# Two recurrent attention layers with feed-forwards: softmax ends, query copies, value rows and the last feed-forward at other places

## The chip, the cores and the metric

The kernel runs on one core of one Trainium2 chip. A core has five engines that work at the same time, each through its own list of instructions in order: TensorE (PE, matmuls and transposes; its weight loads are listed as PEld), VectorE (DVE), ScalarE (ACT), GpSimd (POOL) and SyncE (SP, which here only issues DMA transfers). SBUF is the working memory with 128 partitions; PSUM is the small memory of eight banks into which PE writes and from which DVE and ACT copy results away. The metric is the device time of one execution in microseconds (us).

## What is computed

Two layers, each a memory-augmented attention over 64 segments of 32 tokens followed by a feed-forward with gated ReLU. The attention of a segment sees eight memory rows and the segment's own rows, and its first eight output rows are the memory of the next segment, so the segments of a layer form a chain.

```python
def _A_ref(x, mem0, Wq, Wk, Wv, Wo, seg_len):      # S=2048, Dm=448, H=16, Dh=256, M=8
    mem = mem0
    for s in range(n_seg):                         # 64 segments
        h = jnp.concatenate([mem, x[:, s*seg_len:(s+1)*seg_len]], axis=1)
        q, k, v = (jnp.einsum('btd,dhe->bhte', h, W) for W in (Wq, Wk, Wv))
        scores = jnp.where(mask, jnp.einsum('bhqe,bhke->bhqk', q, k) * scale, -1e9)
        o = jnp.einsum('bhqk,bhke->bhqe', _softmax(scores), v)
        o = jnp.einsum('bhte,hed->btd', o, Wo)
        mem = o[:, :M]
        outs.append(o[:, M:])
    return jnp.concatenate(outs, axis=1)
def _B_ref(x, W_gate, W_up, W_down):               # F=1792
    return (relu(x @ W_gate) * (x @ W_up)) @ W_down
for _ in range(2):
    x = x + _A_ref(_layernorm(x), mem0, Wq, Wk, Wv, Wo, seg_len)
    x = x + _B_ref(_layernorm(x), W_gate, W_up, W_down)
```

## The kernel before

**Preamble (lines 260 to 388).** Both layers use the same weights, so the kernel first multiplies them together once: A_sb = Wq·Wkᵀ for each head (the first loop over p, eight rounds) and B_sb = Wv·Wo (the second loop, eight rounds). The natural weight blocks `nat` come by DMA from SP's queue (`load_nat`), are transposed by PE (`flips`, bank `tpw`) and copied to SBUF by DVE or ACT, whichever `share` picks. The Wo blocks come from POOL's queue; POOL also clears A_sb's unused rows, `nat`'s, and the query tiles before that. A row of 448 features is three chunks of 128 and a fourth of 64 rows; the fourth chunks of two heads are packed into one 128-row chunk in places (`kd` = 3).

**Steps (lines 613 to 876).** Each of the 69 calls of `step` handles one segment of each layer. The second layer's chain (c=1) runs four segments (LAG) behind the first's (c=0): steps 0 to 3 and 64 to 67 have one chain, steps 4 to 63 have both, side by side in the matmuls' columns (80 = two times 40), and step 68 only finishes the output of segment 67. The 16 heads are worked as two halves hf=0 and hf=1. In a step PE

- projects the queries (`project`, matmuls prj): 28 tiles in five banks, in the order of BANKS, tiles 0–5, 6–11, 24–27, 12–17, 18–23. Each bank is copied to SBUF by ACT or DVE: four of them into TQ (here TQ0, TQ6, TQ12, TQ18 by their first tile) and tiles 24–27 into TZ, whose rows 0–63 and 64–127 are two copies of their own. The line that picks the engines is 556 to 559; `busy` is true for all of half hf=1 and, for hf=0, in feed steps;
- multiplies queries with keys: Sm, the scores of the memory's queries (`scores_m`), and Sx, those of the segment's queries (`scores_x`), one of each per half. Sm of hf=1 reads TQ and TZ of hf=1;
- waits for the softmax, which `softmax` splits in three parts: [0] maximum and difference on DVE, [1] the exponential on ACT, [2] the sum, the reciprocal and the product into PM or PX on DVE. m0, m1, x0, x1 are the softmaxes of Sm and Sx for the halves;
- transposes PM and PX (`flipped`, bank pps, copied to PT), multiplies with the keys' rows (`weigh_m` into ya and yb, `weigh_x` into y) and copies into Y;
- multiplies Y with B_sb (`project_out`, 84 ox matmuls per half, and `project_last`, 56 o matmuls of 64 columns).

Every odd step from 3 to 67 carries a `Feed`: layernorm, gate and up products (gps, ups), their product hh and the down product (dps) of one block of 64 rows of each layer. Step 68 is followed by the last one. Steps with a `Feed` are called feed steps, the others no-feed steps.

**Order.** PE's instructions run in the order of the program (`in_order`), and from line 881 on DVE's and ACT's do too (`InOrder`, line 96): what stands behind a waiting instruction waits with it. The PSUM banks are given out by `bank`, which takes the one that a simple clock expects to be free first. Almost all DVE and ACT instructions carry line 96 (or 151 and 153 where they are copies outside it) and all matmuls line 138 in the profile, so that groups are told apart by tile names.

Of the kernel before, what the change touches and what calls it, by code (L numbers as in the profile page):

```python
# [8 lines left out]
BF = mybir.dt.bfloat16  # L9
# [50 lines left out]
def build_kernel(ctx, tc, A_x, A_mem0, A_Wq, A_Wk, A_Wv, A_Wo, B_W_gate, B_W_up, B_W_down, out,  # L60
# [101 lines left out]
    nc.sync.dma_start(xp[1][:], x_dram[0:128])  # L162

    ident = glob.tile([P, P], BF, name="ident")
    make_identity(nc, ident[:])
# [94 lines left out]
    with tc.tile_pool(name="pre", bufs=6) as pre:  # L260
# [4 lines left out]
        for i in range(6):  # L265
            t = pre.tile([P, 4, 512], BF, name=f"nat{i}", bufs=1)
            (nc.gpsimd if i % 2 else dve).memset(t[64:128, 3, :], 0.0)
            nats.append(t)
        nc.gpsimd.memset(A_sb[64:128, 3, :, :, :], 0.0)
        nc.gpsimd.memset(A_sb[0:64, 3, :, 6:24, :], 0.0)  # L270
        for t in TQ + TZ + PX + PM + YB:
# [3 lines left out]
        def load_nat(src, p, eng):  # L275
            t = nats[nn[0] % 6]
            nn[0] += 1
            cols = slice(512 * p, 512 * (p + 1))
            eng.dma_start(t[:, 0:3, :], src[0:384, cols].rearrange("(k p) n -> p k n", p=P))
            eng.dma_start(t[0:64, 3, :], src[384:448, cols])  # L280
            if src is Wq:
                eng.dma_start(t[64:128, 3, :], src[384:448, cols])
            return t

        spent = {dve: 0.0, act: 0.0}

        def share(dst, src, n, per):
            cost = {dve: 60 + n * per[0], act: 170 + n * per[1]}
            eng = min(cost, key=lambda e: spent[e] + cost[e])
            spent[eng] += cost[eng]  # L290
            evac(eng, dst, src)

        def flips(src, p, name):
            nat = load_nat(src, p, nc.sync)
            o = pre.tile([P, 4, 512], BF, tag="tT", name=name)

            def half(e2):
                tp = bank([P, 2, 512], BF, "tpw")
                for e in range(2):
                    for kd in range(4):  # L300
                        tr(tp[:, e, kd * 128:(kd + 1) * 128],
                           nat[:, kd, (2 * e2 + e) * 128:(2 * e2 + e + 1) * 128], ident[:])
                share(o[:, 2 * e2:2 * e2 + 2, :], tp[:], 1024, (0.6, 0.82))

            return o, [lambda: half(0), lambda: half(1)]
# [10 lines left out]
        def first_rows(xn0):  # L316
# [9 lines left out]
            set_mem(0, mem0T[:].unsqueeze(2), (0,))  # L326

        ready, todo = queue(0)
        for u in todo:
            u()  # L330
# [35 lines left out]
        for p in range(NP):  # L366
            hf, p4 = divmod(p, 4)
            vT = ready
            ready, todo = flips(Wv, p + 1, "vT") if p + 1 < NP else (None, [])
            wo = pre.tile([P, 4, DM], BF, tag="wo", name="wo", bufs=4)  # L370
            nc.gpsimd.dma_start(wo[:], Wo[:, 4 * p:4 * p + 4, :])
            for eo in range(2):
                for kd in range(3):
                    bps = bank([P, 512], F32, "bps")
                    for t in range(2):
                        e = 2 * eo + t
                        mm(bps[:, 0:DM], vT[:, e, kd * 128:(kd + 1) * 128], wo[:, e, :],
                           start=(t == 0), stop=(t == 1))
                    share(B_sb[:, hf, tidx(kd, eo, p4), 0:DM], bps[:, 0:DM], DM, (1.28, 0.85))
                    if kd == 1 and todo:  # L380
                        todo.pop(0)()
            bps = bank([P, 512], F32, "bps")
            for t in range(2):
                for eo in range(2):
                    e = 2 * eo + t
                    mm(bps[64 * eo:64 * eo + 64, 0:DM], vT[:, e, 384:448], wo[:, e, :],
                       start=(t == 0), stop=(t == 1), tile_position=(0, 64 * eo))
            share(B_sb[:, hf, 24 + p4, 0:DM], bps[:, 0:DM], DM, (1.28, 0.85))
# [45 lines left out]
    class Feed:  # L434
# [38 lines left out]

        def gate_up(self, u):
            n = self.n
            k = min(4, FT - 4 * u)
            for W_sb, ps in zip((Wu_sb, Wg_sb), self.ps[u]):
                for e in range(k):
                    f = 4 * u + e
                    for kd in range(3):  # L480
                        mm(ps[:, e, n], W_sb[:, kd, f * 128:(f + 1) * 128], xT[:, kd, n],
                           start=False, stop=(kd == 2), skip_group_check=True)
                let_go(ps)
            ups, gps = self.ps[u]
            ut = p_ut.tile([P, 4, 128], BF, tag="ut")
            act.copy(ut[:, 0:k, n], ups[:, 0:k, n])
            dve.scalar_tensor_tensor(out=hh[:, 4 * u:4 * u + k, n], in0=gps[:, 0:k, n], scalar=0.0,
                                     in1=ut[:, 0:k, n], op0=ALU.max, op1=ALU.mult)

        def down(self):  # L490
            i = self.i
            dps = bank([P, 512], F32, "dps")
            for f in range(FT):
                mm(dps[:, 0:DM], hh[:, f, :], Wd_sb[:, f, :], start=(f == 0), stop=(f == FT - 1))
            if self.first:
                dve.tensor_tensor(self.nx[TB:P, :], dps[TB:P, 0:DM], self.x[TB:P, :], op=ALU.add)
                self.st = row_stats(self.nx)
                nc.sync.dma_start(xa[(i + 2) % 3][0:TB, :], self.nx[TB:P, :])
            if self.second:
                dve.tensor_tensor(self.x[0:TB, :], dps[0:TB, 0:DM], self.x[0:TB, :], op=ALU.add)  # L500
                nc.sync.dma_start(out_dram[block(i - LAG // BLK)], self.x[0:TB, :])
# [36 lines left out]
    def project(hf, chains, hb, j, banks, pre={}, busy=False, first=None, inside=None):  # L538

        n = L * len(chains)  # L540
        for i0, k in banks:
# [12 lines left out]
            if i0 < 24:  # L554
                T = TQ[hf][:].rearrange("p g u w -> p g (u w)")[:, :, 16 * i0:16 * (i0 + k)]
                parts = [(act if (i0 != 6 if busy and hf else i0 % 12) else dve, slice(0, P), T)]
            else:
                parts = [(act if busy else dve, slice(0, 64), TZ[hf][0:64, :, 0:64]),
                         (act, slice(64, 128), TZ[hf][64:128, :, 64:128])]
# [53 lines left out]
    def step(g, ff, pre, late):  # L613
# [5 lines left out]
        cols = [(0, 32) if c == 0 else (48, 80) for c in xs] + [(32, 40) if c == 0 else (40, 48) for c in ms]  # L619
        lo, hi = min(a for a, _ in cols), max(b for _, b in cols)  # L620
        end = g == nsteps - 1
        if g == nsteps:
# [3 lines left out]
        def ox_open():  # L626

            nonlocal ox
            ox = bank([P, 3, W], F32, "ox", 1400, hold=True) if not end else None

# [43 lines left out]
        def weigh_x(hf, hk, PT):  # L674
# [14 lines left out]
            for c in chains:  # L689
                keep(act if c == 0 else dve, c, 0, y1[c][:])  # L690
            y2 = {c: bank([P, 384], F32, f"y2_{c}", 1300) for c in chains}
# [9 lines left out]
            for c in chains:  # L701
                eng = dve if c or len(chains) == 1 else act
                keep(eng, c, 16, y2[c][:, 0:256])
                keep(eng, c, 24, y2[c][:, 256:384])

        def project_out(hf, t0, t1):

            if end:
                return
            for t in range(t0, t1):  # L710
# [5 lines left out]
        def project_last():  # L716

            if end:
                return
            o3 = bank([P, W], F32, "o3", 1200)  # L720
# [26 lines left out]
        def finish():  # L747
# [5 lines left out]
            if g == nsteps:  # L753
                act.copy(OT[:, 0:3, 0:SEG], ox[:, :, XO[1]:XO[1] + SEG])
                dve.tensor_copy(OT[:, 0:3, SEG:TB], ox[:, :, XL:XL + SEG])
                return
# [9 lines left out]
        if not chains:  # L766
            late()
            ox_open()
# [12 lines left out]
        if ff is not None:  # L781
            ff.norm()
        pre1 = {}
        if late is not None:
            pre1 = project_early(1, chains, hb, j)
            late()
# [32 lines left out]
        x1 = scores_x(1)  # L819
        x0[0]()  # L820
        if ff is not None:
            ff.open_rows((0, 1))
# [26 lines left out]
        else:  # L849
# [3 lines left out]
            m1[2]()  # L853
            late_flip = 23 if len(chains) == 2 else 26
            project_out(0, 0, late_flip)
            pm = flipped(PM[1], 1, "m1") if ms else None
            x0[2]()
            project_out(0, late_flip, NT)
            weigh_m(1, hk, pm)
            x1[0]()  # L860
            x1[1]()
            next_piece()
            project_last()
            x1[2]()
            project_out(1, 0, 10)
# [4 lines left out]
            project_out(1, 25, NT)  # L870
        if not end:
            finish()
        nxt = active(g + 1)
# [7 lines left out]
    dve.on = act.on = True  # L881
    pre, late = {}, None
    for g in range(nsteps + 1):
        if g == LAG - 1:
            set_mem(LAG, mem0T[:].unsqueeze(2), (1,))
        i = (g - 3) // 2
        pre, late = step(g, Feed(i) if g % 2 and 0 <= i < nblk + LAG // BLK - 1 else None, pre, late)

    ff = Feed(nblk + LAG // BLK - 1)
    ff.residual()  # L890
    ff.norm()
    ff.xposed()
    ff.xposed_out()
    for us in ((0, 1), (2, 3)):
        ff.open_rows(us)
# [61 lines left out]
```

## Time and profile before

| | us |
|---|---|
| three runs | 1611.59, 1609.84, 1609.4 (median 1609.84) |
| the profiled execution | 1608.87 |
| its span in the trace | 1606.8 |
| first loop of the preamble (A_sb) | about 9 to 49 |
| second loop (B_sb) | about 49 to 79 |
| 60 two-chain steps, in 30 pairs of a no-feed and a feed step | 45.58 per pair |
| last no-feed step and last `Feed` | 1581 to 1607 |
| mean granted PE clock | 0.995 of full |

The profile's page gives for each engine the busy time and its share of the span, then groups of instructions by line and tile, and the chain of work that ended last. Busy time is a sum over instructions, a chain is a path through them: an engine with a low share can still stand on the path. The granted clock is the share of full speed that PE is given; where it is 0.5 each matmul takes about twice its time. In a timeline, "[0.40 <-PE prj L138]" says that the engine stood idle 0.40 us before this row and that PE's prj ended the wait. Rows such as "x2" stand for two instructions one after the other.

### The profile page before, as it was taken

Reading aid. Unit: us, or ns where it says so; the run is one execution under the profiler, and the core shown is the slowest. Engines: PE = TensorE matmul, PEld = TensorE weight load, DVE = VectorE, ACT = ScalarE, POOL = GpSimd, SP = SyncE. Lnnn points to the kernel's source line nnn. Section 1 sums busy time; section 2 is a strip of 40 time slices with the busy share of each in tenths; the row PEclk is TensorE's granted clock in tenths of the full one; section 3 lists DMA queues with packets and bytes.
Section 4 is the critical chain, followed back from the end, with each engine's and each line's share of the span. In section 5 each row is a group of like instructions: output and inputs, shape, how many; then the busy total and the mean of one; then the engine's idle time right before and its main releaser. Section 6 shows DMA issues by size and latency. Waiting matters only on the chain.

```text
span 1606.8 us, 89746 instructions
## 1 busy us (share of the span) xinstructions
PE 1583.5 (99%) x41152; PEld 1453.7 (90%) x41152; DVE 1135.4 (71%) x3721; ACT 753.7 (47%) x2057; POOL 87.8 (5%) x176
## 2 busy tenths in 40 slices
PE   8999999999999999999999999999999999999997
PEld 6698899999999999999999999999999999999886
DVE  7766777777677777776777777767777777766774
ACT  5744444554444444544445445444444455444432
POOL 6200000000000000000000000000000000000000
PEclk9989999999999999999999999999999999999999
DMA  9430000000000000000000000000000000000000
GB/s 262 131 108 25 8 9 9 4 9 10 9 9 9 9 9 7 7 9 10 9 9 9 9 9 4 10 9 9 9 9 9 9 5 8 9 8 7 6 7 6
DMA packets 26778, 33.11 MB, mean 21 GB/s; under 512 B 3352, under 2 KB 24736, under 8 KB 26400
## 3 DMA queue, kind: packets, MB, share of 16 engines
q1 hardware_dynamic: 25312, 23.70, 5.3%
q8 instruction: 321, 5.26, 1.4%
q0 software_dynamic: 1088, 3.68, 0.8%
q14 instruction: 57, 0.47, 0.1%
HBM read 23.70 MB, written 1.84 MB: 16 GB/s over the span
## 4 chain that ended last, share of the span: by engine, by line
PE 92%; DVE 5%; POOL 2%; issue 1%; ACT 0%; POOLq 0%; ACTq 0%
PE prj L138 30%; PE ox L138 24%; PE ups L138 7%; PE dps L138 6%; PE gps L138 5%; PE y L138 4%; PE o L138 4%; PE Sx L138 3%; PE pps L146 2%; PE Sm L138 2%; PE bps L138 1%; DVE Y L96 1%; PE kps L146 1%; PE tps L146 1%; PE tpw L146 1%; PE aps L138 1%
## 5 line engine op out<-in xcount | busy, mean ns | idle before, releaser
L138 PE MATMUL prj<-hT,A_sb 128*128 128x80 bf16 (+3 forms) x15232 | 542.2, 199 | 0.0
L138 PEld LDWEIGHTS <-A_sb 128*128 128x128 bf16 (+1 forms) x15232 | 499.6, 99 | 21.9 <-issue 0.6
L138 PEld LDWEIGHTS <-B_sb 128*128 128x128 bf16 (+1 forms) x15232 | 494.6, 103 | 19.2 <-issue 5.7
L138 PE MATMUL ox<-Y,B_sb 128*128 128x80 bf16 (+4 forms) x11424 | 439.2, 199 | 0.0
L96 ACT CAST TQ<-prj 128x480 bf16<-128x480 f32 (+1 forms) x380 | 180.5, 496 | 82.3 <-PE prj L138 75.5
L96 DVE CAST Y<-y 128x256 bf16<-128x256 f32 (+2 forms) x400 | 160.9, 457 | 45.7 <-PE y L138 45.4
L96 ACT CAST Y<-y 128x256 bf16<-128x256 f32 (+1 forms) x368 | 128.4, 420 | 92.5 <-PE y L138 92.5
L96 ACT ACTIVATE se<-se 128x80 f32<-128x80 f32 (+1 forms) x270 | 81.9, 303 | 185.6 <-DVE se L96 181.5
L138 PE MATMUL gps<-xT,Wg_sb 128*128 128x128 bf16 (+3 forms) x1904 | 134.6, 216 | 0.0
L138 PE MATMUL ups<-xT,Wu_sb 128*128 128x128 bf16 (+3 forms) x1904 | 133.2, 217 | 0.5 <-DVE xT L96 0.5
L96 DVE CAST TQ<-prj 128x480 bf16<-128x480 f32 (+1 forms) x228 | 128.6, 573 | 5.8 <-PE prj L138 5.3
L96 ACT CAST TZ<-prj 64x320 bf16<-64x320 f32 (+2 forms) x264 | 97.8, 381 | 40.1 <-PE prj L138 23.5
L96 DVE SCALAR_TENSOR_TENSOR hh<-gps,ut 128x512 bf16<-128x512 f32 (+2 forms) x136 | 80.5, 593 | 50.2 <-PE ya L138 40.0
L138 PEld LDWEIGHTS <-hk 40*128 40x128 bf16 (+1 forms) x1950 | 100.3, 96 | 14.7 <-issue 2.1
L138 PEld LDWEIGHTS <-Wu_sb 128*128 128x128 bf16 (+1 forms) x1904 | 105.7, 97 | 8.0
L138 PEld LDWEIGHTS <-Wg_sb 128*128 128x128 bf16 (+1 forms) x1904 | 107.5, 97 | 0.5 <-issue 0.5
L96 ACT COPY os<-o 64x16 f32<-64x16 f32 (+3 forms) x135 | 25.7, 190 | 165.3 <-PE o L138 164.0
L96 DVE TENSOR_REDUCE ssum<-se 128x2 f32<-128x80 f32 (+1 forms) x270 | 73.3, 272 | 38.3 <-ACT se L96 38.3
L138 PE MATMUL dps<-Wd_sb,hh 128*128 128x448 bf16 x476 | 95.7, 353 | 0.0
L222 POOL TENSOR_SCALAR rstd<-mv 128x1 f32<-128x1 f32 x67 | 14.8, 221 | 1465.3 <-DVE mv L96 1465.3
L138 PEld LDWEIGHTS <-TQ 128*128 128x128 bf16 x1938 | 87.1, 97 | 6.5 <-ACT TQ L96 1.1
L138 PE MATMUL y<-PT,hk 40*128 40x256 bf16 (+1 forms) x1280 | 90.4, 249 | 0.8 <-ACT Y L96 0.6
(116 smaller groups left out, 1939.5 us busy)
## 6 DMA issues: line engine op xcount, KB each, us to landing
wo<-in_A_Wo_dram POOLq DMA_DIRECT2D x8, 448.0 KB, 5.7
nat<-in_A_Wq_dram SPq DMA_DIRECT2D x8, 384.0 KB, 5.4
nat<-in_A_Wk_dram SPq DMA_DIRECT2D x8, 384.0 KB, 5.0
nat<-in_A_Wv_dram SPq DMA_DIRECT2D x8, 384.0 KB, 4.9
xa<-in_A_x_dram SPq DMA_DIRECT2D x32, 56.0 KB, 2.6
xa<-xp SPq DMA_DIRECT2D x32, 56.0 KB, 1.9
out_dram<-xa SPq DMA_DIRECT2D x32, 56.0 KB, 2.0
xp<-in_A_x_dram SPq DMA_DIRECT2D x30, 56.0 KB, 2.4
```

Source lines behind the costliest of these rows:

```text
L96: r = f(*a, **k)
L138: in_order(nc.tensor.matmul(out, lhsT, rhs, **k))
L146: in_order(nc.tensor.transpose(out, src, idn))
L222: nc.gpsimd.tensor_scalar(out=rstd[:], in0=mv[:, 1:2], scalar1=EPS, scalar2=None, op0=ALU.add)
```

## The change

- **Query copies.** In half hf=1 of every step tiles 6–11 (TQ6) are copied by ACT instead of DVE, and TZ's lower rows by DVE instead of ACT. Half hf=0 is as before.
- **Softmax ends.** In no-feed steps x0[2] moves from before the last ox matmuls of hf=0 to after x1[1], and x1[2] from behind `project_last` to ahead of it.
- **One-chain steps.** In step 0 the fourth chunks' projections of both halves are now made ahead of time (`project_early`), as in the other steps; copies of y go to ACT or DVE in another way where there is one chain; `late_flip` is chosen by the width of ox.
- **Step 0.** ox has columns from 0 on (40 columns) instead of the eight memory columns alone.
- **Preamble.** Eight matmuls on a tile of zeros ahead of the first transposes, and four more between those of Wq and Wk. The last 64 rows of Wv are loaded beside those of Wk into rows 64–127 of the fourth chunk, transposed with them and kept in `v3`; Wv's own blocks then need three transposes per 128 columns instead of four. The `nat` blocks are not cleared any more, and of A_sb only rows 64–127 of tiles 24–27. `share` counts when the engines will be free by the simple clock.
- **End.** Step 67 makes gate and up of units 0 and 1 only, and all of its remaining attention work. Units 2 and 3 and the down product of its `Feed` come after step 68, the down product in two parts, around the last `Feed`'s residual and row statistics. The last `Feed` multiplies its down product as pairs of column tiles (even f into rows 0–63 of the bank, odd f into rows 64–127), and the two halves are added after a copy by ACT.

```diff
+        def keep_warm(n):
+            junk = bank([P, 512], F32, "junk")
+            for _ in range(n):
+                mm(junk[:], still[:, 0:128], still[:], start=True, stop=True)
...
-            (nc.gpsimd if i % 2 else dve).memset(t[64:128, 3, :], 0.0)
...
-        nc.gpsimd.memset(A_sb[64:128, 3, :, :, :], 0.0)
-        nc.gpsimd.memset(A_sb[0:64, 3, :, 6:24, :], 0.0)
+        nc.gpsimd.memset(A_sb[64:128, 3, :, 24:NT, :], 0.0)
...
+            if src is Wv:
+                return t
             eng.dma_start(t[0:64, 3, :], src[384:448, cols])
-            if src is Wq:
-                eng.dma_start(t[64:128, 3, :], src[384:448, cols])
+            eng.dma_start(t[64:128, 3, :], (Wq if src is Wq else Wv)[384:448, cols])
...
+                n = 3 if src is Wv else 4
                 for e in range(2):
-                    for kd in range(4):
+                    for kd in range(n):
                         tr(tp[:, e, kd * 128:(kd + 1) * 128],
...
+                if src is Wk:
+                    share(v3[:, p, 2 * e2:2 * e2 + 2, :], tp[:, :, DM:512], 128, (0.6, 0.82))
...
+        keep_warm(8)
         ready, todo = queue(0)
-        for u in todo:
+        for k, u in enumerate(todo):
+            if k == 2:
+                keep_warm(4)
             u()
...
-                    mm(bps[64 * eo:64 * eo + 64, 0:DM], vT[:, e, 384:448], wo[:, e, :],
+                    mm(bps[64 * eo:64 * eo + 64, 0:DM], v3[:, p, e, :], wo[:, e, :],
...
+        def down_part(self, f0, f1):
+            if f0 == 0:
+                self.dps = bank([P, 512], F32, "dps", hold=True)
+            dps = self.dps
+            for f in range(f0, f1):
+                if self.first:
+                    mm(dps[:, 0:DM], hh[:, f, :], Wd_sb[:, f, :], start=(f == 0), stop=(f == FT - 1))
+                else:
+                    r = slice(64 * (f % 2), 64 * (f % 2) + 64)
+                    mm(dps[r, 0:DM], hh[:, f, 0:TB], Wd_sb[:, f, :], start=(f < 2), stop=(f >= FT - 2),
+                       tile_position=(0, r.start), skip_group_check=True)
...
+            if self.second and not self.first:
+                other = main.tile([P, DM], F32, tag="other", name="other")
+                act.copy(other[0:TB, :], dps[TB:P, 0:DM])
+                dve.tensor_tensor(self.x[0:TB, :], dps[0:TB, 0:DM], self.x[0:TB, :], op=ALU.add)
+                dve.tensor_tensor(self.x[0:TB, :], other[0:TB, :], self.x[0:TB, :], op=ALU.add)
...
-                parts = [(act if (i0 != 6 if busy and hf else i0 % 12) else dve, slice(0, P), T)]
+                parts = [(act if busy and hf or i0 % 12 else dve, slice(0, P), T)]
             else:
-                parts = [(act if busy else dve, slice(0, 64), TZ[hf][0:64, :, 0:64]),
+                parts = [(act if busy and not hf else dve, slice(0, 64), TZ[hf][0:64, :, 0:64]),
                          (act, slice(64, 128), TZ[hf][64:128, :, 64:128])]
...
+        if g == 0:
+            lo = 0
...
             for c in chains:
-                keep(act if c == 0 else dve, c, 0, y1[c][:])
+                keep(act if c == 0 or len(chains) == 1 else dve, c, 0, y1[c][:])
...
-                eng = dve if c or len(chains) == 1 else act
+                eng = (act if hf else dve) if len(chains) == 1 else dve if c else act
...
             if g == nsteps:
-                act.copy(OT[:, 0:3, 0:SEG], ox[:, :, XO[1]:XO[1] + SEG])
+                dve.tensor_copy(OT[:, 0:3, 0:SEG], ox[:, :, XO[1]:XO[1] + SEG])
...
-        pre1 = {}
+        pre1 = project_early(1, chains, hb, j)
         if late is not None:
-            pre1 = project_early(1, chains, hb, j)
             late()
...
+        if end:
+            ff.open_rows((0, 1))
+            x0[1]()
+            x1[0]()
+            x1[1]()
+            x0[2]()
+            ff.products(0)
+            ff.products(1)
+            px0 = flipped(PX[0], 2, "x0", act)
+            x1[2]()
+            ff.gated(0)
+            ff.gated(1)
+            weigh_x(0, hk, px0)
+            px1 = flipped(PX[1], 2, "x1", act)
+            weigh_x(1, hk, px1)
+            return {}, None
...
-            late_flip = 23 if len(chains) == 2 else 26
+            late_flip = 23 if hi - lo == W else 26
             project_out(0, 0, late_flip)
             pm = flipped(PM[1], 1, "m1") if ms else None
-            x0[2]()
             project_out(0, late_flip, NT)
             weigh_m(1, hk, pm)
             x1[0]()
             x1[1]()
+            x0[2]()
+            x1[2]()
             next_piece()
             project_last()
-            x1[2]()
...
-    pre, late = {}, None
+    pre, late = project_early(0, active(0), hTb[0], 0), None
...
     ff = Feed(nblk + LAG // BLK - 1)
+    fed.open_rows((2, 3))
     ff.residual()
+    for u in (2, 3):
+        fed.products(u)
+    for u in (2, 3):
+        fed.gated(u)
+    fed.down_part(0, 8)
     ff.norm()
+    fed.down_part(8, FT)
     ff.xposed()
     ff.xposed_out()
+    fed.down_out()
     for us in ((0, 1), (2, 3)):
```

More of the change, by code (lines that the diff above doesn't have):

```diff
@@ L162, in build_kernel @@
     nc.sync.dma_start(xp[1][:], x_dram[0:128])
+    still = glob.tile([P, 512], BF, name="still")
+    nc.vector.memset(still[:], 0.0)
+    def keep_warm(n):
+        junk = bank([P, 512], F32, "junk")
+        for _ in range(n):
+            mm(junk[:], still[:, 0:128], still[:], start=True, stop=True)
     ident = glob.tile([P, P], BF, name="ident")
@@ L279, in load_nat @@
             eng.dma_start(t[:, 0:3, :], src[0:384, cols].rearrange("(k p) n -> p k n", p=P))
+            if src is Wv:
+                return t
             eng.dma_start(t[0:64, 3, :], src[384:448, cols])
-            if src is Wq:
-                eng.dma_start(t[64:128, 3, :], src[384:448, cols])
-            return t
-        spent = {dve: 0.0, act: 0.0}
+            eng.dma_start(t[64:128, 3, :], (Wq if src is Wq else Wv)[384:448, cols])
+            return t
+        v3 = pre.tile([P, NP, 4, 64], BF, name="v3", bufs=1)
+        until = {dve: 0.0, act: 0.0}
         def share(dst, src, n, per):
             cost = {dve: 60 + n * per[0], act: 170 + n * per[1]}
-            eng = min(cost, key=lambda e: spent[e] + cost[e])
-            spent[eng] += cost[eng]
+            ends = {e: max(until[e], now[0]) + cost[e] for e in cost}
+            eng = min(ends, key=ends.get)
+            until[eng] = ends[eng]
             evac(eng, dst, src)
@@ L298, in half @@
                 tp = bank([P, 2, 512], BF, "tpw")
+                n = 3 if src is Wv else 4
                 for e in range(2):
-                    for kd in range(4):
+                    for kd in range(n):
                         tr(tp[:, e, kd * 128:(kd + 1) * 128],
                            nat[:, kd, (2 * e2 + e) * 128:(2 * e2 + e + 1) * 128], ident[:])
-                share(o[:, 2 * e2:2 * e2 + 2, :], tp[:], 1024, (0.6, 0.82))
+                n = DM if src is Wk else 128 * n
+                share(o[:, 2 * e2:2 * e2 + 2, 0:n], tp[:, :, 0:n], 2 * n, (0.6, 0.82))
+                if src is Wk:
+                    share(v3[:, p, 2 * e2:2 * e2 + 2, :], tp[:, :, DM:512], 128, (0.6, 0.82))
             return o, [lambda: half(0), lambda: half(1)]
@@ L474, in gate_up, with products @@
         def gate_up(self, u):
+            self.products(u)
+            self.gated(u)
+        def products(self, u):
             n = self.n
@@ L483, in gate_up, with gated @@
                 let_go(ps)
+        def gated(self, u):
+            n = self.n
+            k = min(4, FT - 4 * u)
             ups, gps = self.ps[u]
@@ L488, in gate_up, with down_out @@
                                      in1=ut[:, 0:k, n], op0=ALU.max, op1=ALU.mult)
+        def down_part(self, f0, f1):
[9 more added lines that the diff above has]
+                       tile_position=(0, r.start), skip_group_check=True)
+            if f1 == FT:
+                let_go(dps)
         def down(self):
[L491 to L494, printed above, removed]
+            self.down_part(0, FT)
+            self.down_out()
+        def down_out(self):
+            i, dps = self.i, self.dps
             if self.first:
@@ L498, in down @@
                 nc.sync.dma_start(xa[(i + 2) % 3][0:TB, :], self.nx[TB:P, :])
-            if self.second:
+            if self.second and not self.first:
[3 more added lines that the diff above has]
+                dve.tensor_tensor(self.x[0:TB, :], other[0:TB, :], self.x[0:TB, :], op=ALU.add)
+                nc.sync.dma_start(out_dram[block(i - LAG // BLK)], self.x[0:TB, :])
+            elif self.second:
                 dve.tensor_tensor(self.x[0:TB, :], dps[0:TB, 0:DM], self.x[0:TB, :], op=ALU.add)
@@ L628, in ox_open @@
             nonlocal ox
-            ox = bank([P, 3, W], F32, "ox", 1400, hold=True) if not end else None
+            ox = bank([P, 3, W], F32, "ox", 1400, hold=True)
         def hk_make():
@@ L706, in project_out @@
         def project_out(hf, t0, t1):
-            if end:
-                return
             for t in range(t0, t1):
@@ L716, in project_last @@
         def project_last():
-            if end:
-                return
             o3 = bank([P, W], F32, "o3", 1200)
@@ L766, in step @@
         if not chains:
-            late()
             ox_open()
@@ L870, in step @@
             project_out(1, 25, NT)
-        if not end:
-            finish()
+        finish()
         nxt = active(g + 1)
@@ L886, in build_kernel @@
         i = (g - 3) // 2
-        pre, late = step(g, Feed(i) if g % 2 and 0 <= i < nblk + LAG // BLK - 1 else None, pre, late)
+        if g % 2 and 0 <= i < nblk + LAG // BLK - 1:
+            fed = Feed(i)
+            pre, late = step(g, fed, pre, late)
+        else:
+            pre, late = step(g, None, pre, late)
     ff = Feed(nblk + LAG // BLK - 1)
+    fed.open_rows((2, 3))
     ff.residual()
+    for u in (2, 3):
[3 more added lines that the diff above has]
+    fed.down_part(0, 8)
     ff.norm()
+    fed.down_part(8, FT)
     ff.xposed()
     ff.xposed_out()
+    fed.down_out()
     for us in ((0, 1), (2, 3)):
```

## The prediction

> **What bounds the kernel now.** I read the busy shares first, then the chain of waits by engine, then the timeline of one pair of steps, and last the two ends of the run.
>
> ```profile
> PE 1583.5 (99%) x41152; PEld 1453.7 (90%) x41152; DVE 1135.4 (71%) x3721; ACT 753.7 (47%) x2057; POOL 87.8 (5%) x176
> ...
> PE 92%; DVE 5%; POOL 2%; issue 1%; ACT 0%; POOLq 0%; ACTq 0%
> ```
>
> TensorE (PE) is busy for 99% of the span and carries 92% of the chain. It works in program order, so a change gains by fewer matmuls, by a faster clock, or by a shorter wait, and it loses by whatever makes PE wait. Between 89 and 1575 us the same two steps repeat: a no-feed step and a feed step, together 45.58 us, 30 times over. The place that decides this change is the last part of the query copies of half hf=1, here in a no-feed step (start, duration, engine, operation):
>
> ```profile
> 1428.15 0.27 ACT L96 ACTIVATE se<-se 128x80 f32<-128x80 f32 x1
> 1428.82 0.86 ACT L96 CAST TZ<-prj 64x320 bf16<-64x320 f32 x2 [0.40 <-PE prj L138]
> 1429.71 1.02 ACT L96 CAST TQ<-prj 128x480 bf16<-128x480 f32 x2
> ...
> 1429.12 0.24 DVE L96 TENSOR_TENSOR PM<-se,rs 128x80 bf16<-128x80 f32 x1
> 1429.28 0.65 DVE L96 CAST TQ<-prj 128x480 bf16<-128x480 f32 x1
> ...
> 1430.66 0.20 PE L138 MATMUL Sm<-hT,TZ 128*128 128x80 bf16 x1
> 1430.78 0.21 PE L138 MATMUL Sm<-hT,TQ 128*128 128x80 bf16 x1
> ```
>
> ScalarE (ACT) copies both halves of TZ and then TQ12 and TQ18. PE's Sm, the score matmuls of this half, starts 1430.78 just behind the end of TQ18 at 1430.73: 0.120 us between its last two matmuls where 0.035 is the usual step. ACT is on the critical path here with no slack, though it is busy only 47% of the span. VectorE (DVE) is held by the softmax end PM until 1429.28.
>
> **The change part by part.**
>
> **1. Query copies, hf=1.** TQ6 goes from DVE to ACT, and TZ's lower half goes from ACT to DVE. Does ACT's upper half then wait for DVE's lower half? The no-feed steps of half hf=0 already split TZ this way, and the view of the tile TZ shows what happens there:
>
> ```profile
> L96 ACT CAST TZ<-prj x264: 178/420/433, 81.9 to 1575.7; 64x320 bf16<-64x320 f32 x105, 64x32 bf16<-64x32 f32 x27
> ...
> L96 DVE CAST TZ<-prj x40: 182/483/483, 81.4 to 1556.7; 64x320 bf16<-64x320 f32 x30, 64x32 bf16<-64x32 f32 x5, 64x128 bf16<-64x128 f32 x5
> ...
>   DVE TZ L96: 14.2, 32
> ```
>
> ACT waited 32 times, 14.2 us in all, and starts 0.035 us after DVE ends. In hf=1 DVE's half stands behind PM, and TQ12 and TQ18 are queued behind the waiting ACT copy. No-feed step: DVE free at 1429.28, TZ lower 0.48 → 1429.77, lag 0.035, TZ upper 0.42 → 1430.22, TQ12 0.56 plus 0.02 → 1430.80, TQ18 0.56 less its 0.10 overlap → 1431.26, PE 0.055 later at 1431.32 instead of 1430.78: **+0.54**. TQ6 itself fits ACT's gap between the exponential at 1428.15 and the TZ bank. Feed step, by the same sum from DVE's 1402.37: 1402.85; 0.09 for ACT's start, since its own bank is late too, and 0.42 → 1403.36; TQ12 1403.94; TQ18 1404.40; PE 1404.455 instead of 1404.015: +0.44, and +0.42 with the lag taken between 0.035 and 0.09: **+0.42**. No trace row has this split in hf=1: if the existing Sm waits (0.085 and 0.137 us) vanish inside the new ones the two are 0.455 and 0.283; a second 0.09 lag makes 0.6 and 0.5.
>
> The Trainium skill, page "PSUM — Partial Sum Buffer", section "PSUM bank collisions raise a hardware error", says two engines may access one bank at the same time if they touch different quadrants of partitions, as rows 0–63 and 64–127 are. By it the two copies could run side by side; this trace shows ACT waiting each time, so the sum takes the wait (the other case is rival A).
>
> **2. Softmax ends in no-feed steps.** x0's second half moves behind x1's first, and x1's second ahead of the 56 matmuls o. Now those matmuls lose time:
>
> ```profile
> 1416.50 1.19 PE L138 MATMUL o<-Y,B_sb 128*64 128x80 bf16 x56
> ...
> 1434.61 1.45 PE L138 MATMUL o<-Y,B_sb 128*64 128x80 bf16 x56
> ...
> 1434.65 0.32 DVE L96 TENSOR_TENSOR PX<-se,rs 128x160 bf16<-128x160 f32 x1
> 1434.90 0.42 DVE L96 CAST Y<-ya 128x256 bf16<-128x256 f32 x1
> ```
>
> 1.45 against 1.19 in the feed step: DVE copies ya to Y only behind PX, and the last o matmuls need Y. With x0's end out of the way the copy runs some 0.3 earlier: **−0.24**. But PX0 is then ready about 1436.76, and its transposes, now at 1437.08 and 0.24 earlier after the change, start 0.15 after PX's end (as in the tail): 1436.91 against 1436.84, so **+0.08** (0 to 0.2).
>
> A pair thus costs 0.54 − 0.24 + 0.08 + 0.42 = +0.80; ×30 = **+24.0 us** (bounds 0.48 and 0.96 a pair: 14 to 29).
>
> **3. One-chain steps** (five no-feed, two feed). The TZ wait costs about +0.53 and +0.52; the earlier projection, the moved ends and the rebalanced Y copies take about 0.36 off a no-feed step: 5×0.16 + 2×0.52 = **+1.8** (−1 to +4).
>
> **4. Preamble.** PE's first work waits 5.5 us for the first weights and runs at half clock until 11.3; eight junk matmuls of 512 columns fill that wait: −0.9. The A_sb memsets on GpSimd (POOL), 6.06 + 3.93 us, become about 0.9: the stall behind them at 16.64 (PE restarts at 17.48) goes, −0.6, and one before tps at 26.4, −0.55. SP issues as many DMAs as before. POOL, though, reaches the four Wo loads (448 KB each, before from 23.3) at 13 to 17 us, ahead of Wq/Wk loads on a DMA system already 92–95% busy, and Wk's loads carry 64 KB more: p=4's Wq lands some 1.3 after it is needed: **+1.3** (0 to 4). Phase two drops four of 16 transposes of Wv per p: 8×4×56 ns = **−1.8**. Projecting early in step 0 saves **−0.6**. Last, step 0's ox has eight columns, and the clock drops (columns: us, then busy and count of PE, PEld, DVE, ACT, POOL; clock; DMA share; GB/s):
>
> ```profile
> 86.40:89.80 3.40, 3.22 (x108) 3.02 (x105) 2.63 (x12) 0.92 (x3) 0.00 (x0) 1.00 0.53 160
> 89.80:100.00 10.20, 10.20 (x295) 9.58 (x293) 4.97 (x20) 3.70 (x14) 0.00 (x0) 0.50 0.37 116
> 106.90:117.10 10.20, 9.94 (x372) 9.32 (x370) 6.53 (x28) 4.99 (x20) 0.00 (x0) 1.00 0.26 71
> ```
>
> The same stretch takes 10.46 us in step 0 and 8.24 in step 1, which has 40 columns and full clock; step 0 gets 40: **−2.2** (0 to −2.4). Together −0.9 −0.6 −0.55 +1.3 −1.8 −0.6 −2.2 = **−5.4** (−9 to −0.5).
>
> The Trainium skill, "TensorE: Matmul & The Clock Gate", section "What's actually happening", has the clock fall after an idle window of about 3.4 us. PE was issuing without a break ahead of the drop, so by that rule wider columns need not help and the sum would be 2.2 higher; the two rows above speak for the columns.
>
> **5. Tail.** The second half of the feed-forward in step 67 (0.28 + 1.05 + 2.65 us of PE, less its waits) moves under the last row statistics, where PE now idles and then runs cold:
>
> ```profile
> 1591.54 0.40 PE L146 MATMUL otp<-ident,OT 128*128 128x128 bf16 x4 [0.68 <-DVE OT L96]
> ...
> 1594.69 0.44 PE L146 MATMUL tps<-ident,xn 128*128 128x128 bf16 x4 [2.75 <-DVE xn L96]
> ...
> 1595.10:1598.40 3.30, 2.79 (x59) 2.72 (x59) 0.85 (x2) 0.39 (x2) 0.00 (x0) 0.50 0.00 0
> ```
>
> Step 68's ox then starts at 1581.8 instead of 1584.69: −2.9. OT's copies side by side: −0.1. The clock stays up over gate and up: −1.2 at most, taken as −0.9. The last down as seven pairs of column tiles: −1.2, against an added ACT copy and a second add, +0.65: −0.55. Together **−4.4** (−6 to −2.5).
>
> **Sum**: 24.0 + 1.8 − 5.4 − 4.4 = **+16.0 us**, made against the profiled execution of 1608.87 (span 1606.8 and 2.1 around it): 1624.9. That execution lies 0.97 under the median of the runs, 1609.84, to which my forecast is put: **1625.8 us**.
>
> **Rivals.**
> *A, the halves run side by side.* Then no wait is added, the copies are merely balanced and the pair keeps −0.24 + 0.08 = −0.16: −4.9 − 0.8 − 5.4 − 4.4 = −15.5, **1594 us**. For it: the halves are different rows of bank and tile. Against it: 32 waits on just this pair of copies. Chance 0.12; this is the rival on the other side, and it decides once ACT's wait per step falls below 0.3 us.
> *B, half the delay is absorbed*, because DVE and ACT catch up while PE stands and the later waits of the pair shrink: 12 + 1.8 − 9.8 = +4, **1614**, down to no change. Against it: beside those counted, PE shows hardly a wait in the pair that could shrink. Chance 0.13, of which 0.05 within 0.2%.
> *C, Wo's early loads hold up Wq by 4 us* instead of 1.3: **1628.5**. For it: in the trace a Wk load issued at 26.90 behind Wo's landed 35.58. Chance 0.12.
> *D, clocks not gained* in step 0 and tail: +2.2 + 0.9, **1629**. Chance 0.13.
>
> **How the numbers follow.** The forecast itself, 1620 to 1628, has 0.50. A measurement of this kernel tells a change from none at about 0.2%, 3.2 us. Faster by more: A, 0.12. Within: 0.05 of B. Slower: 0.83. The range, **1611 to 1631**, leaves out A and the corners of C and D together with the upper bound of part 1. Slower cases hold most of it, so it has one side.
>
> **What would show it.** Right: ACT's TZ row with DVE TZ as its releaser about 100 times instead of 32, Sm's last matmul in each pair late by some half microsecond, o's 56 matmuls at 1.19 in both steps, a pair of about 46.4 us. Wrong: a pair of 45.4 or less (A); PE waiting for nat between 24 and 30 us for more than 2 us (C); clock 0.50 after 89 us or in the last gate and up (D).

## The result and the profile after

The changed kernel takes 1623.69 us (median of four runs, 1623.19 to 1626.59) where the kernel before took 1609.62 beside it: a ratio of 1.0089 with a 95% interval of 1.0071 to 1.0106. The profiled execution took 1623.19, its span is 1621.1: 14.3 us more than the 1606.8 of before. The page's busy shares and the chain of waits by engine:

```profile
PE 1587.5 (98%) x41132; PEld 1448.0 (89%) x41132; DVE 1122.7 (69%) x3706; ACT 751.4 (46%) x2090; POOL 77.7 (5%) x172
...
PE 73%; DVE 15%; ACT 7%; issue 2%; POOL 2%; DMA 1%; SPq 0%; ACTq 0%; POOLq 0%
```

PE has twenty matmuls fewer and still carries less of the chain, 73% instead of 92%: the path now runs through DVE and ACT in every step. The view of the tile TZ, and who waited for it:

```profile
L96 ACT CAST TZ<-prj x188: 181/422/434, 82.6 to 1594.8; 64x320 bf16<-64x320 f32 x150, 64x32 bf16<-64x32 f32 x19, 64x128 bf16<-64x128 f32 x19
...
L96 DVE CAST TZ<-prj x116: 175/476/484, 82.1 to 1594.3; 64x320 bf16<-64x320 f32 x90, 64x32 bf16<-64x32 f32 x13, 64x128 bf16<-64x128 f32 x13
...
  DVE TZ L96: 74.3, 95
```

ACT waits for DVE's half 95 times and 74.3 us in all, where it was 32 times and 14.2. The timelines of ACT, DVE and PE at the same place as before (a no-feed step, hf=1):

```profile
1449.15 0.42 ACT L96 CAST TZ<-prj 64x320 bf16<-64x320 f32 x1 [0.92 <-DVE TZ L96]
1449.60 1.02 ACT L96 CAST TQ<-prj 128x480 bf16<-128x480 f32 x2
...
1448.48 0.24 DVE L96 TENSOR_TENSOR PM<-se,rs 128x80 bf16<-128x80 f32 x1
1448.64 0.47 DVE L96 CAST TZ<-prj 64x320 bf16<-64x320 f32 x1
...
1450.25 0.21 PE L138 MATMUL Sm<-hT,TZ 128*128 128x80 bf16 x1
1450.67 0.21 PE L138 MATMUL Sm<-hT,TQ 128*128 128x80 bf16 x1 [0.21 <-ACT TQ L96]
```

ACT stands idle 0.92 us, TQ12 and TQ18 follow late, and PE's last Sm matmul starts 0.42 us behind the one before it, which itself is 0.23 late; the usual step is 0.035. Over all steps the gaps between these matmuls beyond the usual step have a median of 0.62 us in no-feed and 0.58 in feed steps, where it was 0.09 and 0.14. From the starts of kps, one per step, the no-feed step grew from 18.26 to 18.56 us and the feed step from 27.32 to 27.76. The second part of the change shows in the same step, in PE's and DVE's timelines:

```profile
1454.50 1.19 PE L138 MATMUL o<-Y,B_sb 128*64 128x80 bf16 x56
1456.72 0.29 PE L146 MATMUL pps<-ident,PX 128*128 128x128 bf16 x2
...
1454.50 0.42 DVE L96 CAST Y<-ya 128x256 bf16<-128x256 f32 x1 [0.42 <-PE ya L138]
1456.34 0.32 DVE L96 TENSOR_TENSOR PX<-se,rs 128x160 bf16<-128x160 f32 x1
```

The 56 matmuls o take 1.19 instead of 1.45: the copy into Y is no longer behind PX. The transposes of PX start 0.06 after PX's end. The early part is told by PE's waits of the first 90 us, and by step 0 in the windows (us, then busy and count of PE, PEld, DVE, ACT, POOL; clock; DMA share; GB/s):

```profile
PE tpw L146 <- DMA nat<-in_A_Wk_dram: 3.1, 2, 2.8
...
89.80:100.00 10.20, 9.75 (x352) 9.11 (x352) 5.73 (x24) 5.18 (x20) 0.00 (x0) 1.00 0.41 127
```

PE stood 2.8 us for a block of Wk that had landed behind the Wo loads, while step 0 runs at full clock where it had 0.50. In the tail PE's timeline shows the wait for xn:

```profile
1610.52 0.44 PE L146 MATMUL tps<-ident,xn 128*128 128x128 bf16 x4 [0.27 <-DVE xn L96]
1614.76 1.51 PE L138 MATMUL dps<-Wd_sb,hh 128*64 128x448 bf16 x14
```

It fell from 2.75 to 0.27, and the last down product from 2.81 to 1.51. The 14.3 us by stretch, cut at the kps starts:

| stretch | before | after | difference | forecast |
|---|---|---|---|---|
| start to first kps | 80.56 | 81.30 | +0.7 | −2.5 |
| steps 0 to 3 | 68.96 | 67.07 | −1.9 | −1.8 |
| the two-chain steps (remainder) | | | +21.9 | +24.0 |
| steps 64 to 66 | 56.12 | 54.33 | −1.8 | +0.8 |
| step 67's kps to the end | 35.80 | 31.10 | −4.7 | −4.4 |

### The profile page after: what moved, and what is told of

Same layout as the page of the kernel before. It is cut to its first block, busy times and chain, and to the rows that moved or that the text cites. A ratio compares the mean times of both kernels' runs of the same rounds, so it can differ in the third digit from the quotient of the medians.

```text
span 1621.1 us, 89762 instructions
## 1 busy us (share of the span) xinstructions
PE 1587.5 (98%) x41132; PEld 1448.0 (89%) x41132; DVE 1122.7 (69%) x3706; ACT 751.4 (46%) x2090; POOL 77.7 (5%) x172
## 4 chain that ended last, share of the span: by engine, by line
PE 73%; DVE 15%; ACT 7%; issue 2%; POOL 2%; DMA 1%; SPq 0%; ACTq 0%; POOLq 0%
PE ox L138 25%; PE prj L138 14%; PE ups L138 7%; PE dps L138 5%; PE gps L138 5%; PE o L138 5%; DVE Y L96 4%; ACT TQ L96 4%; PE y L138 3%; ACT TZ L96 2%; PE Sx L138 2%; DVE TZ L96 2%; PE pps L146 1%; DVE rs L96 1%; PE bps L138 1%
## 5 line engine op out<-in xcount | busy, mean ns | idle before, releaser
L138 PE MATMUL ox<-Y,B_sb 128*128 128x80 bf16 (+3 forms) x11424 | 440.1, 199 | 1.3 <-issue 1.3
L96 ACT CAST TQ<-prj 128x480 bf16<-128x480 f32 (+1 forms) x456 | 213.0, 496 | 72.6 <-PE prj L138 68.9
L96 ACT CAST Y<-y 128x512 bf16<-128x512 f32 (+2 forms) x392 | 136.6, 419 | 95.4 <-PE y L138 95.3
L96 DVE CAST Y<-y 128x256 bf16<-128x256 f32 x376 | 151.3, 457 | 42.1 <-PE y L138 41.9
L138 PEld LDWEIGHTS <-TQ 128*128 128x128 bf16 x1938 | 91.8, 97 | 34.0 <-ACT TQ L96 28.1
L96 ACT CAST TZ<-prj 64x320 bf16<-64x320 f32 (+2 forms) x188 | 70.2, 383 | 78.0 <-DVE TZ L96 74.3
L138 PE MATMUL dps<-Wd_sb,hh 128*128 128x448 bf16 (+1 forms) x476 | 93.1, 353 | 0.0
L96 DVE CAST TQ<-prj 128x480 bf16<-128x480 f32 (+2 forms) x152 | 85.8, 573 | 6.2 <-PE prj L138 5.7
```

Source lines behind the costliest of these rows:

```text
L96: r = f(*a, **k)
L138: in_order(nc.tensor.matmul(out, lhsT, rhs, **k))
```

## The experiments

**One part at a time.** Four kernels ask whether ACT's wait is the loss, and whether the two parts of the pair add up. The first turns only the order of the two TZ copies in hf=1:

```diff
                          (act, slice(64, 128), TZ[hf][64:128, :, 64:128])]
+                if busy and hf:
+                    parts.reverse()
```

> The changed kernel with one thing turned: in half hf=1 ACT's copy of TZ's upper rows stands in the program before DVE's copy of the lower rows, so that it has nothing of DVE's to wait for. Theory W (the loss is ACT's wait for DVE, with TQ12 and TQ18 queued behind it): Sm's extra gaps fall from 0.61 and 0.58 us a step to about 0.09 and 0.14, a pair from 46.33 to 45.35, the whole by 30 x 0.98 + 7 x 0.5 = 33 to about 1591 us. Theory L (ACT simply has too much work once TQ6 is its own): the copies are the same ones on the same engines, a pair stays above 46.0 and the time above 1614.

Measured: 1594.5 us (ratio to before 0.9905, 0.989 to 0.992), a pair 45.34. The copies, their number and their engines are those of the changed kernel; 29 us hang on which of two instructions stands first. ACT's and DVE's timelines of a no-feed step:

```profile
1466.13 0.42 ACT L96 CAST TZ<-prj 64x320 bf16<-64x320 f32 x1
1466.70 1.26 ACT L96 CAST TQ<-prj 128x480 bf16<-128x480 f32 x2
...
1466.36 0.24 DVE L96 TENSOR_TENSOR PM<-se,rs 128x80 bf16<-128x80 f32 x1
1466.58 0.48 DVE L96 CAST TZ<-prj 64x320 bf16<-64x320 f32 x1
```

ACT's half is over at 1466.55, when DVE comes free of PM; DVE's half then runs beside ACT's TQ12. In the whole run ACT waits for DVE's half 30 times instead of 95. Theory W holds and L falls. The pair came out within 0.01 of the forecast. The 3.5 us above 1591 lie outside the pairs: the one-chain steps gave 0.2 where I had counted 3.5, and the end of the run took 1.3 more (last section).

The next puts the kernel-before's engines back:

```diff
-                parts = [(act if busy and hf or i0 % 12 else dve, slice(0, P), T)]
+                parts = [(act if (i0 != 6 if busy and hf else i0 % 12) else dve, slice(0, P), T)]
...
-                parts = [(act if busy and not hf else dve, slice(0, 64), TZ[hf][0:64, :, 0:64]),
+                parts = [(act if busy else dve, slice(0, 64), TZ[hf][0:64, :, 0:64]),
```

> The changed kernel with the engine choice for the query copies of the kernel before. Both theories expect the pair to lose the Sm gaps: 46.33 - 0.54 - 0.44 = 45.35, the time about 1591 us. If W holds, this and the kernel with the upper rows first agree within 2 us; if L holds, this one is faster by 20 or more.

Measured: 1594.68 us (0.9902, 0.9886 to 0.9919), a pair 45.35. The two agree to 0.2 us: moving TQ6 to ACT and TZ's lower rows to DVE cost nothing and brought nothing taken together; the order of the two TZ copies made the difference.

The same lines the other way, in the kernel before:

> The kernel before with the new engine choice for the query copies and nothing else. W: a pair 45.58 + 0.53 + 0.44 = 46.55, the whole 30 x 0.97 + 7 x 0.5 = +33 us: 1642. If the delay is partly absorbed in a kernel whose softmax ends stand elsewhere (rival B of the prediction): under 1630.

Measured: 1641.08 us (1.0195, 1.0179 to 1.021), a pair 46.53: +0.95. Nothing of the delay was absorbed in the pairs.

And the softmax ends alone, in the kernel before:

```diff
-            x0[2]()
             project_out(0, late_flip, NT)
             weigh_m(1, hk, pm)
             x1[0]()
             x1[1]()
+            x0[2]()
+            x1[2]()
             next_piece()
             project_last()
-            x1[2]()
```

> The kernel before with x0[2] and x1[2] of the no-feed steps moved and nothing else. By my sum: o's 56 matmuls lose their 0.25 us wait, PX0's transposes wait hardly longer (0.01 in the changed kernel's trace): -0.24 x 30 and some tenths in the one-chain steps, about 1602 us. Rival: without the other wait in front of it PX0 comes too late by the 0.08 that I forecast: 1604.5.

Measured: 1601.0 us (0.9945, 0.993 to 0.996), a pair 45.35: −0.23. Alone the two parts give +0.95 and −0.23, together +0.74; they add up within 0.03. The rival's 1604.5 falls: the four runs lie between 1600.0 and 1601.9.

**Why ACT waits.** DVE and ACT share two things here, the tile TZ they write and the PSUM bank they read. This kernel takes the first away:

```diff
-                         (act, slice(64, 128), TZ[hf][64:128, :, 64:128])]
+                         (act, slice(64, 128), (spare if busy and hf else TZ[hf])[64:128, :, 64:128])]
```

> The changed kernel, but ACT's upper half of TZ in half hf=1 is written to a spare tile, so the upper rows of TZ stay zero and the fourth chunk's part of the scores in that half is left out. DVE and ACT then share no SBUF tile in this place, only the PSUM bank they read. If ACT's wait is for the common bank: it still waits about 0.9 us for DVE's copy and the pair stays at 46.3. If it is for the common tile TZ: the wait is gone and the pair falls to about 45.4.

Measured: 1626.37 us in one execution, a pair 46.31. The view of the tile spare:

```profile
L96 ACT CAST spare<-prj x76: 180/420/421, 86.4 to 1596.7; 64x320 bf16<-64x320 f32 x60, 64x32 bf16<-64x32 f32 x8, 64x128 bf16<-64x128 f32 x8
...
  DVE TZ L96: 60.0, 64
```

64 waits for DVE's copy, 60.0 us: with the common tile TZ gone the wait stays, so what orders the two is the common bank, though they read rows 0–63 and 64–127 of it. (Each prj tile has a bank of its own here, so bank and PSUM tile are not told apart.) The Trainium skill ("PSUM — Partial Sum Buffer", section "PSUM bank collisions raise a hardware error") says that different quadrants of one bank may be accessed together; the kernel as built puts the wait there all the same, and whether the chip would need it was not tried.

**The preamble.** With the upper rows first, and Wo's loads on another queue:

```diff
-            nc.gpsimd.dma_start(wo[:], Wo[:, 4 * p:4 * p + 4, :])
+            nc.sync.dma_start(wo[:], Wo[:, 4 * p:4 * p + 4, :])
```

> The kernel with the upper rows first, and Wo's loads issued from SP's queue behind the blocks of Wq, Wk and Wv instead of from POOL's. If Wo's early loads are what holds up the first loop of the preamble (rival C's mechanism): the 2.8 us wait for nat at 22 to 25 us goes with the cold clock behind it, the first bps starts at about 49 instead of 52.3, and the whole falls by about 3 us, from 1594.5 to 1591. If the 64 KB more in each of Wk's loads are the cause: PE still waits for nat by over 2 us and the first bps stays above 51.5.

Measured: 1591.59 us (0.9879, 0.9863 to 0.9896), the lowest median of all kernels here. The first bps starts at 48.20 instead of 52.29, 4.1 us earlier. PE's waits for nat fall from 3.3 us in all to 0.9, none over 0.5, and the 3.4 us at half clock that followed them (25.4 to 28.8 us) are gone: the Wo loads were the cause, not the 64 KB in Wk's. The 4.1 us belong to these two traces. In the six executions with this preamble and Wo on POOL's queue the first bps came at 49.91 to 52.87, so the price is 1.7 to 4.7 us; it is over 4 in the four in which the clock fell behind the wait. Part of the gain went again: step 1 took 17.19 instead of 15.52. PE stood 1.2 us longer in it with no wait that the profile shows (mostly ahead of ox, 1.16 instead of 0.34), and the clock was at half in its last 1.1 us; why is not shown.

> The kernel with the upper rows first, without the eight and four junk matmuls of the start. My forecast gave them 0.9 us. In the changed kernel the first aps starts at 9.24 as before the change, so they brought nothing up to there; by a warm clock behind it, the fifth aps matmul starts later without them by 0.5 us at least. Rival: the wait for Wq and Wk in DMA sets the start, and first bps moves by under 0.3 us.

The edit takes out `keep_warm(8)` and `keep_warm(4)`. Measured: 1593.83 us in one execution. The first aps starts at 9.97 instead of 9.38 and the fifth 1.45 us later, as expected, but the first bps at 50.02 instead of 52.29. Neither expectation named that: PE comes later to the blocks that are late anyway, waits 0.8 us for those of Wk and Wv instead of 3.0, and the clock does not fall behind the wait. The 50.02 also lies within the 49.91 to 52.87 that came with the junk matmuls. So this did not price them, and a last kernel does it without Wo's loads in the way, the same edit on the kernel with Wo on SP's queue:

> Upper rows first, Wo from SP's queue, and no junk matmuls. Nothing then waits for nat in the first loop but its start, so the value of the junk matmuls shows by itself: the first aps some 0.7 us later than 9.19 and the first bps as much behind 48.20, about 48.9, the whole within 1 us of the kernel with Wo on SP's queue (1591.6). Rival: they had only the DMA to wait for and the first bps stays within 0.2 of 48.20.

Measured: the first aps at 10.16, the first bps at 48.80, 0.60 later. In these two traces the junk matmuls are worth 0.6 us to the end of the first loop, where the forecast had 0.9. The whole was 1593.66 (0.9887, 0.9871 to 0.9904), 2.1 us above the kernel with them and not within 1 as expected, though the two intervals overlap.

**Step 0's columns.**

```diff
-        if g == 0:
-            lo = 0
```

> The kernel with the upper rows first, and step 0's ox with its eight memory columns again instead of 40. By the two rows of the kernel before: the clock falls to 0.50 at about 89 us and step 0 is longer by 2.2 us (2.0 to 2.4). By the rule that the clock falls only behind an idle window: no drop in the clock, step 0 shorter or equal, since each matmul has fewer columns.

Measured: 1594.18 us in one execution. The clock fell, in the windows:

```profile
86.00:88.00 2.00, 1.81 (x69) 1.75 (x67) 1.27 (x7) 0.41 (x2) 0.00 (x0) 1.00 0.71 204
88.00:90.00 2.00, 1.85 (x66) 1.66 (x65) 1.64 (x7) 0.70 (x3) 0.00 (x0) 0.73 0.21 46
90.00:92.00 2.00, 2.00 (x69) 1.95 (x68) 1.04 (x6) 0.65 (x3) 0.00 (x0) 0.50 0.35 106
```

In all four traces with eight columns (the kernel before, the two built on it and this one) the clock falls 9.1 to 10.4 us behind the first kps, and in all eight with 40 it stays at 1.00 there. (In four of the eight it falls later, 15 to 31 us behind the first kps, for 3.4 us.) The length of step 0 alone does not give the price: it took 15.68 here, and with 40 columns 13.89 to 15.29 in seven traces and 16.90 in the eighth, because PE also stands for up to 1.4 us at a time with no wait that the profile shows. Without PE's idle gaps of over 0.15 us, steps 0 and 1 together, over which the low clock extends, take 30.9 us here and 28.1 to 29.4 with 40 columns: 1.5 to 2.8 us. By the Trainium skill ("TensorE: Matmul & The Clock Gate", section "What's actually happening") the clock falls behind an idle window; here PE was busy 1.81 and 1.85 of 2.00 us up to it, and the measurement decides against that reading: thin matmuls were not enough to hold the clock.

**One-chain steps.**

```diff
-                keep(act if c == 0 or len(chains) == 1 else dve, c, 0, y1[c][:])
+                keep(act if c == 0 else dve, c, 0, y1[c][:])
...
-                eng = (act if hf else dve) if len(chains) == 1 else dve if c else act
+                eng = dve if c or len(chains) == 1 else act
```

> The kernel with the upper rows first, and in one-chain steps the copies of y on the engines of the kernel before. With the upper rows first steps 64, 65 and 66 took 16.32, 22.97 and 14.58 us; with the softmax ends alone 16.53, 24.15 and 14.95. If the copies of y on other engines are what I under-valued in the one-chain steps: these three rise by some 0.2, 1.2 and 0.4 us. If not (the earlier projections or the bank order did it): they stay within 0.1.

Measured: 16.33, 24.09 and 15.64 us: +0.0, +1.1 and +1.1 (1594.78 in one execution). In step 65 PM's transposes start 1.18 us behind the matmul before them, and without this edit no such gap is over 0.31. In step 66 the gap there is 0.50; the rest of its +1.1 is time ahead of prj in which PE waited for nothing that the profile shows, and two kernels without this edit have that too (step 66 at 14.95 and 15.01). So the copies of y account for 1.1 us in step 65, some 0.4 in step 66 and nothing in step 64. The kernel before has the gap of step 65 too; in the list of PE's waits from 1535 to 1580 us (total, times, longest) it reads

```profile
PE pps L146 <- DVE PM L96: 1.3, 2, 1.0
```

DVE copied all of chain 1's y for hf=1 ahead of the softmax of m0, and PE waited for PM. With those copies on ACT the wait is gone.

## Why the prediction held, point by point

**The wait of ACT for DVE** was forecast +0.54 in a no-feed step and +0.42 in a feed step. From the gaps between Sm's matmuls it is 0.62 − 0.09 = +0.53 and 0.58 − 0.14 = +0.44, and taken out alone it is worth 0.98 a pair. The forecast rested on two readings above all, the 0.035 us between DVE's and ACT's halves in hf=0 and DVE's release from PM, and both carried over (0.04 in the no-feed step shown). Rival A (the halves side by side) fell, by its own criterion: ACT's wait is 0.9 us a step, not under 0.3. Its time of 1594 us is what the kernel takes once the order is turned (1594.5), in part by luck: the pairs are 2.8 us under its sum there and the preamble 3.2 over. Rival B (half absorbed) fell with the kernel that had the copies alone.

**The softmax ends**: −0.24 forecast, −0.25 measured from the o rows; the new wait of PX0, +0.08, was 0.01. The lag from PX's end to its transposes was taken as 0.15 from the tail; in the pair it is 0.06. A pair came to +0.74 instead of +0.80, 22.3 for thirty instead of 24.0.

**Wo's loads** were mis-sized: +1.3 forecast (0 to 4), 4.1 measured between the two traces by taking them off POOL's queue, 1.7 to 4.7 over all executions. Of the 4.1, 2.4 are waits for nat, and the 3.4 us at half clock behind them fit the rest. This was rival C's mechanism. The gains that it hid were there: with Wo's loads behind, the first loop ends 1.9 us earlier than in the kernel before, where I had −0.9 − 0.6 − 0.55 = −2.05. The second loop gave −1.55 (29.25 to 27.70) against −1.8.

**Step 0**: the clock stayed up as forecast, so rival D fell there, and its 2.2 us lies within the 1.5 to 2.8 of the kernel with eight columns. The stretch of steps 0 to 3 came out at −1.9 against −1.8 forecast, with the one-chain gains of the next point in the balance.

**The one-chain steps** were the term with the wrong sign: +1.8 for all seven, of which +0.84 for steps 64 to 66, measured −1.8 there. I over-sized the TZ wait in them, 0.53 and 0.52 a step or 3.7 in all: the gaps between Sm's matmuls grew by 0.42 in steps 3 and 65, by less in the others and by 1.9 in all seven. And I overlooked what the rebalanced y copies remove: PE's 1.0 us wait for PM stood in PE's list of waits before.

**The tail**: −4.4 forecast, −4.7 measured. From the last prj to the first ox of step 68 −3.15 (−2.9 forecast), gate and up at full clock −1.14 (−0.9), the last down product to the end −0.40 (−0.55).

The errors, +3.3 in the preamble against −2.1 in the pairs and −2.6 in steps 64 to 66, cancelled largely: the total was forecast at +16.0 and is +14.1 between the medians, +14.3 between the spans. That the total came so near is in this part luck; the pairs, which set its sign and size, came out by the mechanism forecast.

## What to carry to other kernels

Here two engines that empty one PSUM bank went one after the other in the order of the program, though their rows differ. Where a trace shows that, let the engine go first that has the critical work queued behind its copy, and let the one that is late anyway wait. An engine at 46% can stand on the path; ask what is next in its queue before giving it a wait. Work taken off a queue moves up whatever stands behind it there: four loads that came early so cost 1.7 to 4.7 us, where the rest of that loop's changes gained 1.9.

## What the runs showed of the hardware that was not expected

The granted clock can fall in one execution and not in another at the same instructions. In step 68 the ox matmuls ran at full clock in the changed kernel, and at half with the upper rows first, where the order of that stretch is the same (windows of the latter):

```profile
1570.40:1572.40 2.00, 2.00 (x52) 1.88 (x51) 0.00 (x0) 1.03 (x3) 0.00 (x0) 0.80 0.04 8
1572.40:1574.40 2.00, 2.00 (x40) 1.95 (x37) 0.00 (x0) 0.00 (x0) 0.00 (x0) 0.50 0.00 0
```

The stretch from step 67's kps to the end was 31.0 to 31.2 us in four traces and 32.4 to 32.9 in five, 1.3 to 1.9 us for a drop that began under full PE load, 0.8 to 1.5 us behind the second of two waits of 0.5 us for PT that all nine have. The Trainium skill ("TensorE: Matmul & The Clock Gate", section "What's actually happening") has the activity judged in windows of about 3.4 us that run freely, whatever the kernel does; the traces agree. In each of the twelve every change of the granted clock lies a whole number of 3.413 us behind the first one; in the kernel before the changes are at 11.30, 89.80, 100.04, 1595.08, 1598.49 and 1605.32 us. Counted on this grid, the second wait for PT ends 1.89 to 2.61 us behind an edge in the five traces with the drop, and 0.91 to 1.80 or 3.32 in the four without: so far as nine traces can tell, the drop hangs on where the window's edge falls.

The start varied too: with the same preamble the first aps came at 9.24 to 10.84 us and the first bps at 49.91 to 52.87. The 10.84 is the one execution in which the clock rose at 10.43 and not at 4.2 to 6.0, and the two first bps under 51 are those in which it did not fall at 25 to 27 us. Differences under 2 us between whole runs of these kernels say little; the median pair, cut from the traces, is 45.34 to 45.35 us in all eight kernels that have the changed softmax ends and no wait of ACT in hf=1, though a single step can be longer by some tenths.
